# Five weight pieces' lower parts made by TensorE, three short units' lower parts all on VectorE, and a smaller DMA scratch for GpSimd

## The chip, the core and the metric

One core of a Trainium2 chip runs the whole program. The metric is the device time of one execution in microseconds (us): 898.3 us for the kernel before, the median of three runs (898.18, 898.3 and 901.01). One further execution was taken by the hardware profiler; all rows come from that one.

Engines are named as in the profile: PE is TensorE's matmul and PEld its weight load, DVE is VectorE, ACT is ScalarE, POOL is GpSimd, SP issues most DMAs.

## What is computed

Three layers follow each other: a linear attention with a complex decay, a feed-forward layer, and a mixture of 8 experts of which each token takes one.

```python
for t in range(S):                                  # B, H, S, D = 4, 8, 768, 48
    S_re, S_im = ar*S_re - ai*S_im + k[t] v[t]^T, ar*S_im + ai*S_re
    y[:, :, t] = einsum('bhd,bhde->bhe', q[t], S_re)
x = y.transpose(0, 2, 1, 3).reshape(3072, 384)
h = x @ w_in                                        # 384 -> 2048
x = (max(h, 0) + alpha * min(h, 0)) @ w_out         # 2048 -> 384
e = argmax(x @ w_gate + modality_bias[modality_id]) # 8 experts
out[token] = gate * (max(x @ w1[e], 0) @ w2[e])     # 384 -> 1024 -> 384
```

The feed-forward weights come as 64-bit floats and are put together from their two halves on the chip.

## The kernel before

**Two parts per number.** The two feed-forward layers multiply in a format narrower than float32 (F32R). Each operand is split: an upper part (rounded by a copy on ACT) and a lower part (the operand less the upper part). A product is the sum of three matmuls: upper by upper, upper by lower, lower by upper.

**Weight pieces.** `w_in` and `w_out` are cut into 16 pieces of 128 hidden channels, fc = 0 to 15, each 128 x 768: 384 columns of `w_in` and 384 of `w_out`. A piece is loaded as raw bits (`wraw`), decoded by three DVE instructions (L624, L627, L630) into a working buffer (`wf`), copied to the upper part by ACT (L577), and subtracted by DVE to give the lower part (L578). PE transposes the `w_out` half into a PSUM bank (`pl`, L582), ACT copies it out (L586), and `weights_gate` multiplies it by `w_gate` (`og`, L596). There are four working buffers, chosen by fc % 4, so piece fc + 4 can be decoded only when all readers of piece fc are done. The banks for `pl`, `og` and the attention's `py` and `pu` are given out in turn from one pair (`pq0`, `pq1`).

**Attention.** A step k (24 of them, 128 time steps of one batch row) begins with `polar`: magnitudes, angles and three running scans on DVE and ACT, ending in the rows `z` (L785, L787). These are written to DRAM and read back in another layout (`zd`, `qk`); then PE multiplies (`pa`, `pk`, `py`, `pu`, L818 to L850). Two steps make a unit.

**First feed-forward layer** (`moe1`). For each of 12 units, 8 groups p of two pieces: `ph` on PE (L887, L888 upper, L890 with the weights' lower part), the activation `n` (ACT L895, DVE L897), its upper part `gh` (ACT L900), its lower part `gl` (DVE L875), then `acc` (PE L930). Below, `ph0_4` is group 4 of unit 0. There are two `ph` banks, so a group can begin only when `n` of the group two before it is done.

**Order at the start.** Two strings set the order in which the parts of the first units are written. START is run before `moe1` begins, TURN has one entry for each of its first turns. A letter is a step: x, y, q, p are single instructions of `polar` of steps 0, 1, 2-3 and 4-5; A, a, B and C are parts of attention; D decodes two pieces and F makes their parts; f is four matmuls on the identity that fill PE's time (L191); < and > begin and end a stretch in which each step's DVE instructions are chained behind the last. A scheduler then places the instructions on each engine's queue; every queue runs in order.

**Experts** (`moe2`). The tail of the program. Tokens are gathered by POOL (L377), multiplied unit by unit and scattered by POOL (L413). A unit has 8 steps f; step f needs 768 columns of weights, loaded into one of a few buffers (`wr`, four here), copied by ACT (`wh`, L485) and subtracted for the lower part (`wl`, L486): by POOL for f = 0, 3, 6 and by DVE for the others. Units of 128 x nt tokens: four with nt = 4 (`s`), one with nt = 3 (`t`), three with nt = 2 (`f`, the last). `hh` and `hl` are the two parts of the hidden values (L504, L505), `ptf` the transposes at the head of the next unit (L390).

Of the kernel before, what the change touches and what calls it, by code (L numbers as in the profile page):

```python
# [11 lines left out]
F32 = mybir.dt.float32  # L12
F32R = mybir.dt.float32r
# [3 lines left out]
ALU = mybir.AluOpType  # L17
PSUM = bass.MemoryType.PSUM

B, H, S, D = 4, 8, 768, 48  # L20
# [3 lines left out]
DM, FF = 384, 2048  # L24
# [3 lines left out]
F2 = 8  # L28
# [6 lines left out]
NEARLY = 4  # L35
NFINAL = 3
NTRIP = 1
START = 'x3 y2 x3 y3 x y x y x y3 < x3 y2 x < x4 > x2 y > x3 < x y2 < x2 q b y10 c w A2 a A > r f a A f a f a < > q f2 q8 f2 q5 D F q3 r f q2 f q9 f q3 f q4 D d'
TURN = ('B', 'D2 B F2 B > B2 D F B', 'B2 D F2 L', '', 'D', 'D F p', '', 'p3 F', '<2 p > p2', 'p > p3 < p3 > p11', 'p7', '', 'p4 < C3', 'C3 >2 s >', 'C p C')
GHB = 3  # L40
ATB = 2
LEAD = 3
# [57 lines left out]
class Emit:  # L100
# [26 lines left out]
    def consts(self):  # L127
        nc, cp = self.nc, self.cp
        self.tiny = cp.tile([128, 1], F32, name="tiny")
        nc.vector.memset(self.tiny, 1e-25)  # L130
        warm = cp.tile([128, 1], F32, name="warm")
        nc.scalar.activation(warm, self.tiny, AF.Abs_reciprocal_sqrt)
        self.trig = cp.tile([128, 1], F32, name="trig")
        self.ident = cp.tile([128, 128], F32, name="ident")
        make_identity(nc, self.ident)
        self.mask = cp.tile([128, 128], F32, name="mask")
        nc.gpsimd.memset(self.mask, 1.0)
        nc.gpsimd.affine_select(
            out=self.mask, in_=self.mask, pattern=[[1, 128]], compare_op=ALU.is_ge,
            fill=0.0, base=0, channel_multiplier=-1,  # L140
        )
        self.hpi = cp.tile([128, 1], F32, name="hpi")
        nc.gpsimd.memset(self.hpi, math.pi / 2)
        self.mth = cp.tile([128, 1], F32, name="mth")
        nc.gpsimd.memset(self.mth, -0.56)

        self.first = {}
        for nm, at0, rest in (("angle", 0.0, 1.0), ("inverse", 1.0, 1e18), ("decay", 1.0, 0.0)):
            t = self.first[nm] = cp.tile([128, 3 * CH], BF16, name=f"first_{nm}")
            nc.gpsimd.memset(t, rest)  # L150
            nc.gpsimd.memset(t[:, ::CH], at0)
        self.carry = cp.tile([128, B, 3], F32, name="carry")
        self.magic = cp.tile([128, 1], F32, name="magic")
        nc.gpsimd.memset(self.magic, MAGIC)

        self.oks = cp.tile([128, NSTEP], F32, name="oks")
        nc.gpsimd.memset(self.oks, 2.0 * 3 * CH)
        self.pend = cp.tile([128, NSTEP, 3], F32, name="pend")
        self.state = cp.tile([96, B * H * D + 16], F32, name="state")
        nc.gpsimd.memset(self.state[:, B * H * D:], 0.0)  # L160
        self.al1 = cp.tile([128, NFC], F32, name="al1")
        one = self.one = cp.tile([128, 1], F32, name="one")
        nc.gpsimd.memset(one, 1.0)
        self.mhalf = cp.tile([128, 1], F32, name="mhalf")
        nc.gpsimd.memset(self.mhalf, -0.5)
        self.ones = one.to_broadcast([128, CH])
        self.small = cp.tile([128, NFC], F32, name="small")
        nc.gpsimd.memset(self.small, 0.0)
# [251 lines left out]
    def moe2(self, units):  # L420


        n = len(units)
        regs, heads, turned, accs, ws, hs, gates = {}, {}, {}, {}, {}, {}, {}

        def head(j):
            if j < n:
                nm, get, nt, known = units[j]
                regs[j] = get()
                heads[j] = self.unit_head(nm, regs[j][1], nt, known)  # L430

        def load(i):
            j, f = divmod(i, F2)
            if j < n:
                ws[i] = self.ffn_load(units[j][0], regs[j][0], f)

        def turn(j):
            if j < n:
                turned[j] = self.unit_turn(units[j][0], units[j][2], heads[j][1])

        def l2(i):
            j, f = divmod(i, F2)
            nm, _, nt, _ = units[j]
            if f == 0:
                accs[j] = self.ffn_acc(nm, nt)
            self.ffn_l2(nt, f, hs.pop(i), accs[j])
            if f == F2 - 1:
                self.unit_out(nm, nt, heads.pop(j)[0], gates.pop(j), accs.pop(j))

        head(0)  # L450
        for i in range(PF):
            load(i)
        yield
        turn(0)
        yield
        for i in range(n * F2):
            j, f = divmod(i, F2)
            nm, _, nt, _ = units[j]
            if f == HD:
                head(j + 1)  # L460
            load(i + PF)
            hs[i] = self.ffn_l1(nm, nt, f, ws.pop(i), turned[j])
            if f == GT:
                gates[j] = self.unit_gate(nm, nt, heads[j][1])
            if f == F2 - 1:
                turn(j + 1)
            for k in {0: [i - 1], 1: [], F2 - 1: [i - 2, i - 1]}.get(f, [i - 2]):
                if k >= 0:
                    l2(k)
            yield  # L470
        l2(n * F2 - 1)
        yield
# [1 line left out]
    def ffn_acc(self, nm, nt):  # L474
        return [self.pq.tile([128, DM], F32, name=f"a2{nm}_{t}", tag="a2", bufs=4) for t in range(nt)]

    def ffn_load(self, nm, e, f):

        nc, hp = self.nc, self.hp
        raw = hp.tile([128, 2 * DM], F32, name=f"wr{nm}_{f}", tag="wr", bufs=self.hb[0])  # L480
        nc.sync.dma_start(raw, self.wcat[ds(e, 1), f].rearrange("o p n -> p (o n)"))
        wh = hp.tile([128, 2 * DM], F32R, name=f"wh{nm}_{f}", tag="wh", bufs=self.hb[1])
        wl = hp.tile([128, 2 * DM], F32R, name=f"wl{nm}_{f}", tag="wl", bufs=self.hb[1])
        with self.behind_turn(PM):
            nc.scalar.copy(wh, raw)  # L485
            (nc.vector if f % 3 else nc.gpsimd).tensor_tensor(wl, raw, wh.bitcast(F32), ALU.subtract)  # L486
        return wh, wl

    def ffn_l1(self, nm, nt, f, w, xT):
# [75 lines left out]
    def weights_part(self, *fcs, guard=False):  # L565

        nc = self.nc
        if 0 in fcs:
            self.w, self.wT = [], {}
        ws = [self.tmp(fc) for fc in fcs]  # L570
        yield from self.decode([self.raws.pop(fc) for fc in fcs], ws, guard)
        yield
        for fc, w in zip(fcs, ws):
            p = self.wp.tile([128, 2, WW], F32R, name=f"w{fc}", tag=f"w{fc}")
            self.w.append(p)
            n = 2 * DM
            nc.scalar.copy(p[:, 0, :n], w)  # L577
            nc.vector.tensor_tensor(p[:, 1, :n], w, p[:, 0, :n].bitcast(F32), ALU.subtract)  # L578
            pool, tag, bufs = self.bank()
            pt = pool.tile([128, 512], F32, name=f"pl{fc}", tag=tag, bufs=bufs)  # L580
            for c in range(3):
                nc.tensor.transpose(pt[:, 128 * c:128 * c + 128], w[:, DM + 128 * c:DM + 128 * c + 128], self.ident)  # L582
            if fc % 4 == 0:
                self.wT4 = self.ap_.tile([128, 4, DM], F32, name=f"wT{fc}", tag="z", bufs=ZB)
            wT = self.wT[fc] = self.wT4[:, fc % 4]
            nc.scalar.copy(wT, pt[:, :DM])  # L586
# [584 lines left out]
def body(ctx, tc, aps):  # L1171
# [5 lines left out]
    def polar(*ks):  # L1177
        st = third if ks[0] == 4 else em.polar(ks)
        for k in ks:
            em.load_v(k)  # L1180
        yield
        yield from em.polar_run(st, 0, len(ks), True)
        yield
# [25 lines left out]
    def attn_unit(u):  # L1209
        xts[u] = em.wp.tile([128, 3, 2, 256], F32R, name=f"xt{u}", tag="xt", bufs=XB)  # L1210
        for k in (2 * u, 2 * u + 1):
            yield from em.attn(k, xts[u])
# [78 lines left out]
    def steps(text):  # L1291

        for part in re.findall("([^0-9 ]+)([0-9]*)", text):
            for c in part[0] * int(part[1] or 1):
                if c in "<>":
                    link[0] = c == "<"
                else:
                    with em.behind_turn() if c in PT else nullcontext():
                        (chained if link[0] else step)(c)

    gens["p"], gens["C"] = polar(4, 5), attn_unit(2)
    steps(START)
    jobs, later = {}, {}
# [21 lines left out]

    for g, text in enumerate(TURN):
        first, _, then = text.partition("/")
        at(g, steps, first)
        at(g, steps, then, d=later)
    at(CG, consts, d=later)  # L1330
    shift = {0: 0}
    for u in range(3, NU):
# [153 lines left out]
```

## Time and profile before

| | |
|---|---|
| median of three runs | 898.3 us |
| the profiled execution's own time | 894.0 us |
| its span, first to last instruction | 892.2 us |
| PE, DVE busy | 821.8 us (92%), 669.9 us (75%) |
| ACT, POOL busy | 467.2 us (52%), 205.2 us (23%) |
| mean granted TensorE clock | 0.979 of full speed |

A matmul counts as busy while it streams or waits in the array's pipeline, so a busy PE can still be a slow one. A wait is booked on the engine that idles, with the instruction that ended it.

### The profile page before, as it was taken

To read this page: it belongs to the slowest core of one execution; us is meant where nothing else is said; L and a number is where in the kernel's file an instruction comes from. 1 tells how busy PE (TensorE), PEld (TensorE's weight loads), DVE (VectorE), ACT (ScalarE), POOL (GpSimd) and SP (SyncE) were. 2 spreads that over 40 slices of the span, in tenths; PEclk is the share of its full clock that TensorE was granted. 3 is DMA by queue.
4 is the path that set the end of the run, shared out by engine and by line. 5 is a ranking of instruction groups with operands and counts; after the bars stand their busy time and mean duration, and the time that the engine had idled before them with its cause. 6 is when DMAs were issued, how large, how long until landed. Compare 5 with 4: busy or idle time off the path is not lost.

```text
span 892.2 us, 16224 instructions
## 1 busy us (share of the span) xinstructions
PE 821.8 (92%) x6037; PEld 784.8 (88%) x6037; DVE 669.9 (75%) x1419; ACT 467.2 (52%) x871; POOL 205.2 (23%) x204
## 2 busy tenths in 40 slices
PE   0699998999799999999999999899999999999993
PEld 0688997989799999999999999899988888999893
DVE  7999978999886979797988889355644754656751
ACT  7644466757564656474656554133344445456550
POOL 2001321021120121212121211000332543534640
PEclk9999899999899999999999999899999999999997
DMA  8769203662737253443535262401365477667650
GB/s 337 244 214 329 35 1 107 156 207 72 192 67 192 68 141 119 114 134 100 144 99 126 104 154 95 85 24 27 105 188 144 144 235 257 199 229 268 203 170 20
DMA packets 63591, 130.37 MB, mean 146 GB/s; under 512 B 10456, under 2 KB 39656, under 8 KB 63504
## 3 DMA queue, kind: packets, MB, share of 16 engines
q1 hardware_dynamic: 59536, 119.49, 44.9%
q0 software_dynamic: 3968, 9.77, 3.3%
q8 instruction: 49, 0.80, 0.4%
q14 instruction: 38, 0.31, 0.1%
HBM read 98.17 MB, written 28.91 MB: 142 GB/s over the span
## 4 chain that ended last, share of the span: by engine, by line
PE 53%; DVE 22%; DMA 12%; issue 6%; ACT 3%; POOL 2%; SPq 1%; POOLq 0%; ACTq 0%; DVEq 0%
PE acc L930 12%; PE a2s L516 6%; DMA qk<-zd 6%; PE ph L887 5%; PE ph L888 4%; PE ph L890 4%; PE pa L818 3%; DVE n L897 2%; PE p2s L501 2%; PE p2s L497 2%; PE p2s L498 2%; DMA zd<-z 2%; DVE z L785 2%; PE pu L850 2%; PE py L836 2%
## 5 line engine op out<-in xcount | busy, mean ns | idle before, releaser
L930 PE MATMUL acc<-w,gh 128*128 128x392 f32 x768 | 158.8, 345 | 0.3 <-ACT gh L900 0.3
L887 PE MATMUL ph<-xt,w 128*128 128x256 f32 x576 | 153.8, 295 | 5.2 <-DVE n L897 4.2
L888 PE MATMUL ph<-xt,w 128*128 128x256 f32 x576 | 148.0, 285 | 0.0
L930 PEld LDWEIGHTS acc<-w,gh 128*128 128x128 f32 x768 | 133.7, 190 | 1.0 <-ACT gh L900 0.5
L887 PEld LDWEIGHTS ph<-xt,w 128*128 128x128 f32 x576 | 110.9, 192 | 7.1 <-DVE n L897 4.8
L897 DVE SCALAR_TENSOR_TENSOR n<-n,al,ph 128x256 f32<-128x256 f32 x192 | 84.1, 474 | 42.2 <-ACT n L895 42.1
L888 PEld LDWEIGHTS ph<-xt,w 128*128 128x128 f32 x576 | 111.1, 193 | 0.2 <-issue 0.2
L890 PE MATMUL ph<-xt,w 128*128 128x256 f32 x576 | 102.1, 286 | 0.0
L895 ACT ACTIVATE n<-ph 128x512 f32<-128x512 f32 x96 | 57.0, 594 | 82.1 <-PE ph L890 80.0
L875 DVE TENSOR_TENSOR gl<-n,gh 128x512 fp32r<-128x512 f32 x96 | 66.8, 696 | 31.1 <-ACT gh L900 30.9
L900 ACT CAST gh<-n 128x512 fp32r<-128x512 f32 x96 | 59.2, 617 | 57.9 <-DVE n L897 53.3
L930 PE MATMUL acc<-w,gl 128*128 128x392 f32 x384 | 89.3, 347 | 0.0
L890 PEld LDWEIGHTS ph<-xt,w 128*128 128x128 f32 x576 | 83.5, 192 | 0.0
L279 POOL DMA_INDIRECT tbl<-tok,ix x24 | 27.4, 1143 | 203.1 <-DVE ix L277 193.7
L930 PEld LDWEIGHTS acc<-w,gl 128*128 128x128 f32 x384 | 70.4, 192 | 0.3 <-issue 0.2
L818 PE MATMUL pa<-qk 96*128 96x128 f32 x384 | 54.3, 285 | 13.6 <-DMA qk<-zd 11.7
L818 PEld LDWEIGHTS pa<-qk 96*128 96x128 f32 x384 | 50.1, 197 | 17.4 <-issue 8.9
L505 DVE SCALAR_TENSOR_TENSOR hls<-p2s,hhs 128x512 fp32r<-128x512 f32 x32 | 22.1, 690 | 33.3 <-ACT hhs L504 29.3
L836 PE MATMUL py<-at,v 128*64 128x128 f32 x384 | 42.4, 286 | 2.0 <-DVE at L820 2.0
L516 PE MATMUL a2s<-whs,hhs 128*128 128x384 f32 x128 | 43.8, 342 | 0.0
L516 PE MATMUL a2s<-wls,hhs 128*128 128x384 f32 x128 | 43.5, 340 | 0.0
L485 ACT CAST whs<-wrs 128x768 fp32r<-128x768 f32 x32 | 26.4, 835 | 30.5 <-PE a2s L516 17.1
(363 smaller groups left out, 1898.1 us busy)
## 6 DMA issues: line engine op xcount, KB each, us to landing
zd<-z SPq DMA_DIRECT2D x24, 771.0 KB
qk<-zd SPq DMA_DIRECT2D x24, 771.0 KB
wraw<-in_w_io_dram SPq DMA_DIRECT2D x16, 768.0 KB
wrs<-in_wcat_dram SPq DMA_DIRECT2D x32, 384.0 KB
ck<-in_w_io_dram SPq DMA_DIRECT2D x16, 768.0 KB
wrf<-in_wcat_dram SPq DMA_DIRECT2D x24, 384.0 KB
wa<-in_pa__dram SPq DMA_DIRECT2D x10, 768.0 KB
wq<-in_pq__dram SPq DMA_DIRECT2D x10, 768.0 KB
```

Source lines behind the costliest of these rows:

```text
L279: nc.gpsimd.indirect_dma_start(out=self.tbl, out_offset=bass.IndirectOffsetOnAxis(ap=ix, axis=0), in_=self.tok[:, c, b, :], in_offset=None ...
L516: nc.tensor.matmul(acc[t], x[:, 128 * t:128 * t + 128], w[:, DM:], start=(f == 0 and x is hh and w is wh), stop=(last and x is hl))
L818: nc.tensor.matmul(pa[:, i, :], kt[:, h, :], qt[:, h, :CH], start=True, stop=True)
L836: nc.tensor.matmul(o, v[:, h * D:h * D + 64], ats[g][:, i, :], start=True, stop=(c == 0))
L875: return engine.tensor_tensor(gl, nf, gh.bitcast(F32), ALU.subtract).ins
L887: nc.tensor.matmul(ph[:, i, :], w1(fc, 0, c), xt[:, c, 0, :], start=(c == 0), stop=False)
L888: nc.tensor.matmul(ph[:, i, :], w1(fc, 0, c), xt[:, c, 1, :], start=False, stop=False)
L890: last = nc.tensor.matmul(ph[:, i, :], w1(fc, 1, c), xt[:, c, 0, :], start=False, stop=(c == 2)).ins
L895: nc.scalar.activation(nf, ph, AF.Relu, scale=-1.0)
L897: paced = nc.vector.scalar_tensor_tensor(nf[:, i, :], nf[:, i, :], self.al1[:, 2 * p + i:2 * p + i + 1], ph[:, i, :], ALU.mult, ALU.add).ins
L900: copy = nc.scalar.copy(gh, nf).ins
L930: nc.tensor.matmul(acc[t][:, :XW], x[:, i, 128 * t:128 * t + 128], self.w[2 * p + i][:, h, DM:], start=(p == i == h == 0 and x is gh), sto ...
```

## The change

Four edits. (1) For pieces fc = 3 to 7 the lower part is no longer made by DVE: PE multiplies the piece by the identity (float32, L586 after), adds the upper part times minus identity (F32R, L587 after) into the same bank (`pd`), and ACT copies the difference out (L588 after), in two halves of 384 columns. (2) START and TURN are rewritten. (3) In units with nt under 3 the weights' lower parts for f = 0, 3, 6 are made by DVE too. (4) The SBUF that POOL's DMAs use for descriptors is set to 4096 bytes of a partition.

```diff
-START = 'x3 y2 x3 y3 x y x y x y3 < x3 y2 x < x4 > x2 y > x3 < x y2 < x2 q b y10 c w A2 a A > r f a A f a f a < > q f2 q8 f2 q5 D F q3 r f q2 f q9 f q3 f q4 D d'
+START = 'x2 y x y4 x3 y x2 y x y3 x7 y > x2 < y > x2 y x2 <2 x y3 < x2 q b y2 r y7 c w A2 f a A > r a A f a f a < > q2 f2 q8 f2 q f q3 D F q3 f q8 f q8 f2 q2'
...
+        self.minus = cp.tile([128, 128], F32R, name="minus")
+        nc.gpsimd.tensor_scalar(self.minus, self.ident, -1.0, 0.0, ALU.mult, ALU.add)
...
-            (nc.vector if f % 3 else nc.gpsimd).tensor_tensor(wl, raw, wh.bitcast(F32), ALU.subtract)
+            (nc.vector if f % 3 or nt < 3 else nc.gpsimd).tensor_tensor(wl, raw, wh.bitcast(F32), ALU.subtract)
...
-            nc.vector.tensor_tensor(p[:, 1, :n], w, p[:, 0, :n].bitcast(F32), ALU.subtract)
+            if 3 <= fc < 8:
+                for i in range(2):
+                    cs = slice(DM * i, DM * i + DM)
+                    pool, tag, bufs = self.bank()
+                    pd = pool.tile([128, 512], F32, name=f"pd{fc}_{i}", tag=tag, bufs=bufs)
+                    nc.tensor.matmul(pd[:, :DM], self.ident, w[:, cs], start=True, stop=False)
+                    nc.tensor.matmul(pd[:, :DM], self.minus, p[:, 0, cs], start=False, stop=True)
+                    nc.scalar.copy(p[:, 1, cs], pd[:, :DM])
+            else:
+                nc.vector.tensor_tensor(p[:, 1, :n], w, p[:, 0, :n].bitcast(F32), ALU.subtract)
...
-    nc = _bacc.Bacc("TRN2", target_bir_lowering=False, num_devices=1)
+    nc = _bacc.Bacc("TRN2", target_bir_lowering=False, num_devices=1, dynamic_dma_scratch_size=4096)
```

In the order of the queues, lines past L137 are shifted by up to 12 after the change (L578 is L590, L624 is L636, L818 is L830). A number behind a name is the piece, step or unit.

DVE's queue from attention step 2 on, before:

```order
L820 TENSOR_TENSOR at2_0_550<-pa2_0_545,mask_85 128x512
L578 TENSOR_TENSOR w2_627<-wf2_520,w2_627 128x768
L578 TENSOR_TENSOR w3_635<-wf3_521,w3_635 128x768
L624 TENSOR_SCALAR wf6_605<-wraw6_245 128x768
L624 TENSOR_SCALAR wf7_606<-wraw7_247 128x768
L627 SCALAR_TENSOR_TENSOR wf6_605<-wraw6_245,wf6_605 128x768
L627 SCALAR_TENSOR_TENSOR wf7_606<-wraw7_247,wf7_606 128x768
L630 SCALAR_TENSOR_TENSOR wf6_605<-wraw6_245,wf6_605 128x768
L630 SCALAR_TENSOR_TENSOR wf7_606<-wraw7_247,wf7_606 128x768
L820 TENSOR_TENSOR at2_1_618<-pa2_1_613,mask_85 128x512
L578 TENSOR_TENSOR w4_643<-wf4_597,w4_643 128x768
L578 TENSOR_TENSOR w5_652<-wf5_598,w5_652 128x768
```

and after:

```order
L832 TENSOR_TENSOR at2_0_556<-pa2_0_551,mask_87 128x512
L636 TENSOR_SCALAR wf7_612<-wraw7_249 128x768
L590 TENSOR_TENSOR w2_633<-wf2_526,w2_633 128x768
L639 SCALAR_TENSOR_TENSOR wf7_612<-wraw7_249,wf7_612 128x768
L636 TENSOR_SCALAR wf6_611<-wraw6_247 128x768
L642 SCALAR_TENSOR_TENSOR wf7_612<-wraw7_249,wf7_612 128x768
L639 SCALAR_TENSOR_TENSOR wf6_611<-wraw6_247,wf6_611 128x768
L832 TENSOR_TENSOR at2_1_624<-pa2_1_619,mask_87 128x512
L642 SCALAR_TENSOR_TENSOR wf6_611<-wraw6_247,wf6_611 128x768
L636 TENSOR_SCALAR wf8_771<-wraw8_251 128x768
L636 TENSOR_SCALAR wf9_772<-wraw9_253 128x768
L639 SCALAR_TENSOR_TENSOR wf8_771<-wraw8_251,wf8_771 128x768
```

The subtractions of pieces 3, 4 and 5 are gone from here (those of 6 and 7 from further on), and the decoding of pieces 8 and 9 stands in their place.

PE's queue at the same place, before:

```order
L818 MATMUL pa2_0_545<-qk2_516 128x128 x4
L826 MATMUL pk2_0_552<-ident_80,qk2_516 128x96 x4
L582 MATMUL pl4_646<-ident_80,wf4_597 128x128 x3
L887 MATMUL ph0_2_845<-xt0_151,w4_643 128x256
L582 MATMUL pl5_655<-ident_80,wf5_598 128x128 x3
L826 MATMUL pk2_1_620<-ident_80,qk2_516 128x96 x3
L818 MATMUL pa2_1_613<-qk2_516 128x128 x4
```

and after:

```order
L838 MATMUL pk2_0_558<-ident_80,qk2_522 128x96 x4
L586 MATMUL pd4_0_658<-wf4_603,ident_80 128x384
L587 MATMUL pd4_0_658<-w4_656,minus_85 128x384
L838 MATMUL pk2_1_626<-ident_80,qk2_522 128x96 x3
L830 MATMUL pa2_1_619<-qk2_522 128x128 x4
L838 MATMUL pk2_1_626<-ident_80,qk2_522 128x96
L586 MATMUL pd4_1_662<-wf4_603,ident_80 128x384
L587 MATMUL pd4_1_662<-w4_656,minus_85 128x384
L594 MATMUL pl4_666<-ident_80,wf4_603 128x128 x3
L838 MATMUL pk3_0_720<-ident_80,qk3_524 128x96 x3
L586 MATMUL pd5_0_674<-wf5_604,ident_80 128x384
L587 MATMUL pd5_0_674<-w5_672,minus_85 128x384
```

Each of the five pieces puts four matmuls into PE's queue, between the attention's own, and `pl` of a piece stands behind them.

DVE's queue at the end of `polar` of steps 4 and 5, before:

```order
L897 SCALAR_TENSOR_TENSOR n1_3_1396<-n1_3_1396,al1_109,ph1_3_1377 128x256 x2
L875 TENSOR_TENSOR gl0_6_1402<-n0_6_1347,gh0_6_1351 128x512
L875 TENSOR_TENSOR gl1_3_1454<-n1_3_1396,gh1_3_1400 128x512
L785 TENSOR_TENSOR z4_1373<-wq4_541,x4_1028 128x3x128
L787 TENSOR_TENSOR z4_1373<-wq4_541,x4_1028 128x3x128
```

and after:

```order
L909 SCALAR_TENSOR_TENSOR n1_3_1437<-n1_3_1437,al1_111,ph1_3_1418 128x256 x2
L887 TENSOR_TENSOR gl0_6_1443<-n0_6_1388,gh0_6_1392 128x512
L797 TENSOR_TENSOR z4_1414<-wq4_547,x4_1059 128x3x128
L799 TENSOR_TENSOR z4_1414<-wq4_547,x4_1059 128x3x128
L797 TENSOR_TENSOR z5_1462<-wq4_547,e4_1061 128x3x128
```

`gl1_3` no longer stands ahead of the last two instructions of `z4`.

## Rows read from the trace of the kernel before

**Rows 1.** The page's head: span of the profiled execution.

```profile
span 892.2 us, 16224 instructions
```

**Rows 2.** Stretches of the span: busy time by engine, granted clock, DMA share.

```profile
core 0: us, PE busy (x) PEld busy (x) DVE busy (x) ACT busy (x) POOL busy (x), PEclk, DMA share, GB/s
...
60.00:100.00 40.00, 36.01 (x282) 32.77 (x282) 39.73 (x61) 20.36 (x47) 6.33 (x11) 0.92 0.78 249
100.00:162.00 62.00, 57.14 (x389) 56.12 (x388) 53.95 (x81) 40.52 (x76) 11.94 (x22) 0.94 0.22 64
162.00:660.00 498.00, 483.59 (x3883) 468.01 (x3882) 396.87 (x944) 262.18 (x472) 86.05 (x71) 0.99 0.42 112
...
820.00:892.20 72.20, 56.40 (x390) 54.51 (x389) 34.75 (x67) 30.42 (x63) 29.77 (x21) 0.93 0.41 129
```

**Rows 3.** PE's three largest waits, 60 to 162 us: total, times, longest.

```profile
PE ph L887 <- DVE n L897: 4.2, 1, 4.2
PE py L836 <- DVE at L820: 2.0, 2, 1.6
PE pl L582 <- DVE wf L630: 1.2, 1, 1.2
```

**Rows 4.** Timeline of DVE: start, us, work, and idle time before it in brackets.

```profile
94.18 3.58 DVE L578 TENSOR_TENSOR w<-wf,w 128x768 fp32r<-128x768 f32 x4
...
122.55 0.95 DVE L698 TENSOR_TENSOR m<-m,e 128x768 f32<-128x768 f32 x1
...
141.03 0.46 DVE L897 SCALAR_TENSOR_TENSOR n<-n,al,ph 128x256 f32<-128x256 f32 x1
...
149.31 0.69 DVE L875 TENSOR_TENSOR gl<-n,gh 128x512 fp32r<-128x512 f32 x1 [1.89 <-ACT gh L900]
...
150.39 0.56 DVE L787 TENSOR_TENSOR z<-wq,x 128x384 f32<-128x384 f32 x1
```

**Rows 5.** Timeline of PE.

```profile
51.24 3.80 PE L191 MATMUL fill<-ident 128*128 128x128 f32 x32
...
96.63 2.11 PE L596 MATMUL og<-wg,wT 128*128 128x8 f32 x12
...
141.54 0.45 PE L887 MATMUL ph<-xt,w 128*128 128x256 f32 x1 [4.15 <-DVE n L897]
```

**Rows 6.** The chain that ended last: an F32R stretch, a POOL DMA, attention's way back.

```profile
746.35 2.10 PE a2s L516 x12
...
699.25 3.91 DMA tbl<-tok,ix
...
154.53 6.65 DMA qk<-zd
161.22 1.16 PE pa L818 x8
```

**Rows 7.** ACT's copies out of a bank, by line: ns min/median/max.

```profile
L586 ACT COPY wT<-pl x16: 473/482/496, 55.4 to 117.7; 128x384 f32<-128x384 f32 x16
```

**Rows 8.** PE's waits from 162 us to the end: total, times, longest.

```profile
PE pa L818 <- DMA qk<-zd: 11.7, 6, 5.1
PE ptf L390 <- DVE hlf L505: 2.1, 1, 2.1
```

**Rows 9.** Timelines of POOL, ACT and DVE in the short units.

```profile
831.50 4.38 POOL L486 TENSOR_TENSOR wlf<-wrf,whf 128x768 fp32r<-128x768 f32 x2
...
843.87 1.58 POOL L377 DMA_INDIRECT xgf<-x2d,idsf  x1
...
836.51 0.83 ACT L485 CAST whf<-wrf 128x768 fp32r<-128x768 f32 x1 [3.37 <-DMA wrf<-in_wcat_dram]
...
842.73 1.81 DVE L486 TENSOR_TENSOR wlf<-wrf,whf 128x768 fp32r<-128x768 f32 x1 [1.08 <-ACT whf L485]
...
868.88 0.96 DVE L486 TENSOR_TENSOR wlf<-wrf,whf 128x768 fp32r<-128x768 f32 x1 [1.09 <-ACT whf L485]
```

**Rows 10.** POOL's scatters by line: ns min/median/max.

```profile
L413 POOL DMA_INDIRECT out_dram<-ots,idss x16: 976/1038/1823, 692.1 to 803.3; - x16
```

More of the change, by code (lines that the diff above doesn't have):

```diff
@@ L37 @@
 NTRIP = 1
-START = 'x3 y2 x3 y3 x y x y x y3 < x3 y2 x < x4 > x2 y > x3 < x y2 < x2 q b y10 c w A2 a A > r f a A f a f a < > q f2 q8 f2 q5 D F q3 r f q2 f q9 f q3 f q4 D d'
-TURN = ('B', 'D2 B F2 B > B2 D F B', 'B2 D F2 L', '', 'D', 'D F p', '', 'p3 F', '<2 p > p2', 'p > p3 < p3 > p11', 'p7', '', 'p4 < C3', 'C3 >2 s >', 'C p C')
+START = 'x2 y x y4 x3 y x2 y x y3 x7 y > x2 < y > x2 y x2 <2 x y3 < x2 q b y2 r y7 c w A2 f a A > r a A f a f a < > q2 f2 q8 f2 q f q3 D F q3 f q8 f q8 f2 q2'
+TURN = ('D d B >', 'D2 B F2 B3 > F B D B', 'D L', 'D F2', 'D F', 'p', '', 'p3 F p < p < p', 'p2 >', 'p3 < p2 B p6 > p6', 'p6', 'p3', '< p C3', 'C3 >2', 'C p C s >')
 GHB = 3
@@ L434, in load @@
             if j < n:
-                ws[i] = self.ffn_load(units[j][0], regs[j][0], f)
+                ws[i] = self.ffn_load(units[j][0], regs[j][0], f, units[j][2])
         def turn(j):
@@ L475, in ffn_acc, with ffn_load @@
         return [self.pq.tile([128, DM], F32, name=f"a2{nm}_{t}", tag="a2", bufs=4) for t in range(nt)]
-    def ffn_load(self, nm, e, f):
+    def ffn_load(self, nm, e, f, nt=4):
         nc, hp = self.nc, self.hp
```

## The prediction

> **What bounds the kernel now.** I read the windows first, then PE's waits, then the timelines, and the chain of waits last. The windows [rows 2] show two regimes. From 162 to 660 us PE is busy 483.59 of 498 us while DVE is busy 396.87: PE is the limit, at a clock of 0.99. From 60 to 100 us it is the other way round: DVE is busy 39.73 of 40 us, PE 36.01, and DVE stays close to full to 162 us (53.95 of 62). PE's waits say the same. In 60 to 162 us its largest waits [rows 3] are 4.2, 2.0 and 1.2 us, 7.4 in sum, and all end with a DVE instruction. After 162 us PE waits for attention's rows, six times, 11.7 us [rows 8]. Each such wait is a DMA that starts when DVE has finished `polar`, and stands on the chain [rows 6] (6.65 us of DMA, then `pa` at 161.22). So what moves DVE's work and PE's together at about 160 us moves the end with it, as PE has almost no slack behind.
>
> The tail (820 us on) has one PE wait, 2.1 us, for `hlf` of DVE [rows 8]. Its origin is on POOL [rows 9]: behind scatters and gathers it begins the lower parts of the short units only at 831.50; the raw buffer comes free late, ACT's copy waits 3.37 us for the load into it, and DVE and PE follow.
>
> **The front: pieces 3 to 7 (edits 1 and 2).**
>
> *What DVE loses.* Four of the subtractions take 3.58 us (at 94.18) [rows 4], 0.9 each; one follows the next by some 0.87. Five are 4.35 us. The queue after the change holds the same DVE instructions otherwise, so from attention step 4 on DVE has 4.35 us less ahead of it. The new order gives more to some places: `gl1_3` (at 149.31, 0.69 us after 1.89 us idle) [rows 4] no longer stands ahead of `z4`'s last instruction, and `polar` of steps 4 and 5 (122.55) has some 6 us less work ahead, by the instructions that now stand behind it. What is moved behind is done later, so I count the 4.35 alone. DVE is full where they are taken away, so nothing hides them.
>
> *What PE gains.* Ten float32 products of 384 columns and ten F32R ones. "f2 q8 f2" in START is sixteen identity matmuls of 128 columns; they show as 32 records in 3.80 us [rows 5], two records of 119 ns each, 0.24 us a matmul. Three such are 0.71 us, ten times 7.1. The F32R product is priced by the chain's `a2s`, 12 of 384 columns in 2.10 us [rows 6], 0.175 each, 1.75 in sum. Together 8.9 us. If a float32 product cost only two F32R ones it would be 3.5 + 1.75 = 5.25: the lower bound. I take 8.9, since the fill is the same operation on the same operand types.
>
> *Does PE have room?* From 60 to 162 us PE is busy 36.01 + 57.14 = 93.15 of 102 us [rows 2]. With 8.85 more it would be busy 102.0, which leaves nothing. But the stretch contains time at the lower clock: 0.92 and 0.94 are means of 2.4 and 1.2 GHz, so 40 x 0.08 + 62 x 0.06 = 6.9 us of busy time is there only because the clock was halved. It falls behind the waits named above and behind the 24 products of 8 columns around 95 us, where twelve take 2.11 us [rows 5]. The change spreads those in sixes between larger matmuls, and fills PE's gaps before them with 384-column ones. If all of that clock comes back, PE needs 102.0 - 6.9 = 95.1 us, and a stretch shortened by 4.35 offers 97.65. So it fits, narrowly; I take it that most of the clock returns. The `n` wait of 4.15 us at 141.54 [rows 5] shrinks by as much as DVE comes earlier than PE there.
>
> *What ACT gains.* Ten copies of 128x384 at 0.48 us [rows 7], 4.8 us; ACT is busy 20.36 of 40 us in 60 to 100 [rows 2], so they have room, but each stands between PE's product and the next user of its bank. There are two banks for `pd`, `pl`, `py` and `pu`. Nothing in the trace before shows this hand-off more than once over 0.3 us, so its cost is bounded: nothing below, and above one 0.83 us cast ahead in ACT's queue (at 836.51) [rows 9] and the 0.48 us copy, 1.3 us for each of the ten halves, 13 us. PE has attention's or `ph`'s instructions between most halves, so I take nothing and keep the rest as a rival. A piece's working buffer is now freed by PE rather than DVE, one to three microseconds later; the decoding of the piece four further on waits for it on DVE, with DVE's whole queue behind. At most this adds to the same rival.
>
> The additional fills, 4 matmuls or 0.95 us, lie before `ph` of unit 0 in a place where PE waits for the pieces anyway. `minus` is one early POOL instruction off any path; POOL is 23% busy.
>
> Sum of the front: -4.35 us, with bounds of -7.4 (PE's three waits on DVE go whole) and 0 (PE full, with what goes beyond it among the rivals).
>
> **The tail (edit 3).** The nine lower parts of the three short units go from POOL to DVE. One takes DVE 0.96 us undisturbed (868.88) and POOL about 2.19 (4.38 for two) [rows 9]. On DVE the first is done by about 830, the raw buffer comes free 3 us sooner, and the 2.1 us wait has nothing to end it late. DVE is busy 34.75 of 72.2 us from 820 on [rows 2]; nine more are 8.6, so it has room. I take -2.1; bounds are 0 and -2.5 (the wait and half a microsecond of its wake).
>
> What speaks against this is in the same rows: DVE's lower part took 1.81 us where POOL ran its own beside it (842.73) and 0.96 alone, and POOL's gather took 1.58 us at 843.87, right after. The Trainium skill (SBUF — State Buffer, "SBUF: two separate sides") states why such pairs collide: VectorE with two SBUF inputs and a GpSimd operation that reads SBUF share a port pair as an exclusive lock, and the one that starts second is fully blocked. By that rule the nine subtractions, each now at the head of a unit beside POOL's gathers, would hold those off too; by the row the collision is with POOL's own subtraction, which goes away. The row is what I go by: with two gathers held off by 0.56 us each (1.58 less the 1.02 of an ordinary one, as the scatters of rows 10 have in the median) the tail would come to -1.0 in place of -2.1, and the whole to 893.0, inside A.
>
> **The scratch (edit 4).** It removes and adds no instruction. Where POOL has to wait for descriptors of an earlier transfer, a gather or scatter would start later: the trace before shows them at 0.98 to 1.82 us [rows 10] and a transfer behind one at 3.91 [rows 6]. I take nothing; the upper bound is three unit heads in the tail held by the landing of the transfer before, 3 x 3.91 less some 2 us of slack each (an estimate from PE's step of twelve `a2s`, 2.10 [rows 6]), about +6. It is rival D.
>
> **Sum.** -4.35 - 2.1 = -6.4 us. The profiled execution's own time is 894.0 (span 892.2 [rows 1] and 1.8 around it); it would be 887.6. The median of the runs, 898.3, lies 4.3 above the profiled one; I keep that offset, so the predicted time is 898.3 - 6.4 = **891.9 us**. About 0.3%, or 2.7 us, is what a measurement of this kernel can tell from no change: faster is below 895.6, slower above 901.0.
>
> **The rivals.**
>
> *A, the forecast*: -6.4; its bounds together give 898.3 - 7.4 - 2.5 = 888.4 at the low end, and the tail at -1.0 with half the front 895.1 at the high one. For it: DVE at 39.73 of 40 and three waits on DVE. Against it: PE fits only if the clock returns. Chance 0.56.
>
> *B, PE takes what DVE gives*: PE's 8.9 us are paid by half of the 7.4 us of waits and half of the 6.9 of clock, 7.15, so the front is +1.7 and the tail -2.1: 897.9, no change that can be told. The same time results if the front does not do what it says because PE's waits there end with a load and not with DVE; DMA share is 0.78 from 60 to 100 us [rows 2]. Chance 0.16.
>
> *C, PE becomes the bound* between 64 and 95 us: the products come in before `ph0_3`, the clock does not return, and PE's queue waits at the two banks for ACT's copies. PE: +8.85, less 3.7 of waits filled, tail -2.1, gives +3.0: **901.4**, slower; with all waits left, +6.75 or 905. It decides without any hand-off if no clock returns; if half of the 6.9 us returns, from hand-offs of 3.1 us, 0.3 for each half piece; if all, from 6.5 us, 0.65 each. For it: 102.0 of 102 us. Against it: PE waits 4.2 us in one place after all this, at 137 to 141, and can catch up there. Chance 0.17, of it 0.04 within the bound.
>
> *D, the scratch delays POOL's transfers*: +6 less the rest's -1.0 or so, 903, decided by whether more descriptors are outstanding than it holds. The trace can't exclude it. The Trainium skill (DMA: Bandwidth & Descriptors, "Terms") says that descriptors of GpSimd's transfers are written to rings in SBUF, so fewer bytes are a shorter ring; no run so far shows one full. Chance 0.03.
>
> *E, both effects in full*: all 7.4 us of waits and the idle 1.89 of `gl1_3` go, and PE keeps the full clock to 162 us: -7.4 - 1.9 - 2.1 = -11.4: 886.9. Chance 0.08.
>
> **How the numbers follow.** Faster is A and E, 0.64; same is B (0.15) and 0.04 of C, 0.19; slower is the rest, 0.17. The range of 8 in 10 is from 886.9 (E) to 901.4 (C at its price); what lies outside is D, C beyond its price and the tail of E. A alone is 888.4 to 895.1.
>
> **What would show it.** In the profile after: eleven subtractions in place of sixteen at the line of DVE's lower part; `polar` 4's first instruction (122.55 before) at 115 to 119; `pa` after `zd` (161.22) at 156 to 157; PE's wait for `n` gone or under 2 us; a granted clock above 0.95 in 60 to 100; no wait of `ptf` for `hlf`; no lower parts of `f` units on POOL. The forecast is wrong if PE is at 100% from 64 to 106 us with the clock still low (B or C), if new waits of `pd` or `pl` for ACT sum to over 3 us (C), if `pa` is not before 159 (B), or if POOL's gathers grow past 2 us (D).

## The result, and the profile after

The changed kernel takes **882.65 us** (median of 4 runs, 881.87 to 885.25); the kernel before took 898.24 us beside it (4 runs, 897.81 to 901.01). The ratio is 0.983, with a 95% interval of 0.980 to 0.986: 15.6 us faster. A second series, beside other runs of the kernel before, gave 0.984 (0.981 to 0.988). The forecast was 891.9 with a range of 886.9 to 901.4; the direction was right, and the time lies 4 us below the range.

The profiled execution of the changed kernel has a span of 883.5 us, 8.7 less than before [rows 1]. Its head, then the same stretches as in [rows 2]:

```profile
span 883.5 us, 16307 instructions
```

```profile
core 0: us, PE busy (x) PEld busy (x) DVE busy (x) ACT busy (x) POOL busy (x), PEclk, DMA share, GB/s
60.00:100.00 40.00, 39.20 (x288) 33.93 (x288) 36.28 (x56) 23.74 (x53) 1.57 (x6) 0.96 0.74 249
100.00:162.00 62.00, 61.11 (x453) 59.51 (x452) 57.75 (x89) 44.29 (x85) 22.99 (x26) 1.00 0.29 84
162.00:660.00 498.00, 482.55 (x3871) 467.60 (x3871) 392.75 (x942) 259.62 (x468) 88.93 (x71) 0.99 0.43 111
820.00:883.50 63.50, 55.71 (x391) 54.50 (x389) 38.97 (x75) 30.91 (x63) 16.25 (x13) 0.96 0.47 148
```

The front has changed sides. PE is busy 100.3 of 102 us from 60 to 162 us (93.15 before), at a clock of 0.96 and 1.00 (0.92 and 0.94), and DVE has 3.7 us of idle time in the first stretch, where it had 0.3. PE's waits in 60 to 162 us, which were 7.4 us on DVE in the three largest alone [rows 3], are these, all of them:

```profile
PE pl L594 <- ACT wT L598: 0.6, 1, 0.6
PE ph L899 <- ACT w L579: 0.6, 1, 0.6
PE pa L830 <- DMA qk<-zd: 0.3, 1, 0.3
PE pl L594 <- DVE wf L642: 0.2, 1, 0.2
```

The chain's pieces that answer to the last rows of [rows 6] come 3.6 to 4.2 us sooner: `zd` at 146.80 (151.01), and `pa` at 157.59 (161.22). First the piece of before, then those of after:

```profile
151.01 3.51 DMA zd<-z
```

```profile
146.80 3.51 DMA zd<-z
150.33 7.22 DMA qk<-zd
...
157.59 1.16 PE pa L830 x8
```

The other place is the very end. POOL's last scatter, in its timeline before and after (start, us, in brackets the idle time before it):

```profile
880.20 0.98 POOL L413 DMA_INDIRECT out_dram<-otf,idsf  x1 [0.31 <-issue]
```

```profile
877.40 0.97 POOL L415 DMA_INDIRECT out_dram<-otf,idsf  x1 [0.30 <-issue]
```

Before, the span ran on for 12.0 us from that start (to 892.2); after, for 6.1 (to 883.5). What changed in there is mainly one instruction on POOL's sequencer, which counts as no busy time and stands in none of the rows ahead of the prediction. The program's last line, all instructions of the kind DRAIN on POOL (ns min/median/max), before and after:

```profile
L1482 POOLq DRAIN  x3: 40/107/6123, 885.2 to 891.9; - x3
```

```profile
L1494 POOLq DRAIN  x3: 40/107/978, 881.7 to 883.2; - x3
```

One DRAIN takes 6.12 us before and 0.98 after. The profile's waits show the same time under another name: SP's queue waits 5.6 us "for PE's sequencer" in the closing barrier before, and 0.5 after. PE had long been done; the row of the instruction itself tells it.

**The sum by places** in the two profiles, each from the start of an instruction to that of the next: to the last `acc` by the upper part in the first feed-forward layer, from 656.2 to 653.2, -3.0; from there to the first `a2f` of the short units +3.2 (169.7 to 172.9); the short units -3.0 (51.9 to 48.9); last product to last scatter 0; end -5.9. Together -8.7. The +3.2 belongs to this one execution: its clock is 0.83 from 700 to 720 us. A second profile of the same program was taken to try this; it shows 1.00 there and 170.1 us for the stretch. Its span was 874.4 where 880 to 881 had been expected, so the clock is not all that differs. The spread between executions sits mainly in PE's waits for `qk` after 162 us (11.7 us before, 12.4 after, 7.5 in that second profile), and it doesn't follow the edits: from 7.5 to 13.1 us in seven profiles with the changed front, 10.0 to 11.7 in three with that of before. So below, stages are compared by marks that these waits don't move, and whole times by ratios.

### The profile page after: what moved, and what is told of

It is laid out like the page before. It is cut to its first block, busy times and chain, and to the rows that moved or that the text cites. A ratio compares the mean times of both kernels' runs of the same rounds, so it can differ in the third digit from the quotient of the medians.

```text
span 883.5 us, 16307 instructions
## 1 busy us (share of the span) xinstructions
PE 825.5 (93%) x6075; PEld 786.8 (89%) x6075; DVE 669.1 (76%) x1423; ACT 471.4 (53%) x881; POOL 198.3 (22%) x196
## 4 chain that ended last, share of the span: by engine, by line
PE 63%; DVE 18%; DMA 9%; issue 5%; ACT 2%; POOL 2%; SPq 1%; POOLq 0%; DVEq 0%; ACTq 0%
PE acc L942 14%; PE a2s L518 7%; PE ph L899 5%; DMA qk<-zd 5%; PE ph L902 5%; PE ph L900 5%; PE pa L830 4%; DMA zd<-z 3%; PE p2s L503 2%; PE pu L862 2%; PE p2s L499 2%; PE p2s L500 2%; PE py L848 2%; DVE n L909 2%; PE a2f L518 2%
## 5 line engine op out<-in xcount | busy, mean ns | idle before, releaser
L899 PE MATMUL ph<-xt,w 128*128 128x256 f32 x576 | 151.9, 292 | 2.0 <-issue 0.8
L900 PE MATMUL ph<-xt,w 128*128 128x256 f32 x576 | 146.3, 283 | 0.0
L899 PEld LDWEIGHTS ph<-xt,w 128*128 128x128 f32 x576 | 109.5, 190 | 3.3 <-issue 1.9
L900 PEld LDWEIGHTS ph<-xt,w 128*128 128x128 f32 x576 | 109.6, 190 | 0.2 <-issue 0.2
L902 PE MATMUL ph<-xt,w 128*128 128x256 f32 x576 | 100.8, 283 | 0.0
L942 PE MATMUL acc<-w,gl 128*128 128x392 f32 x384 | 87.2, 342 | 0.0
L902 PEld LDWEIGHTS ph<-xt,w 128*128 128x128 f32 x576 | 82.4, 190 | 0.0
L281 POOL DMA_INDIRECT tbl<-tok,ix x24 | 29.4, 1225 | 202.5 <-DVE ix L279 192.7
L830 PE MATMUL pa<-qk 96*128 96x128 f32 x384 | 54.1, 285 | 15.5 <-DMA qk<-zd 13.2
L830 PEld LDWEIGHTS pa<-qk 96*128 96x128 f32 x384 | 50.3, 197 | 18.9 <-issue 8.8
L832 DVE TENSOR_TENSOR at<-pa,mask 128x512 f32<-128x512 f32 x48 | 32.7, 682 | 12.8 <-PE pa L830 6.3
```

The costliest lines, as they stand in the source:

```text
L281: nc.gpsimd.indirect_dma_start(out=self.tbl, out_offset=bass.IndirectOffsetOnAxis(ap=ix, axis=0), in_=self.tok[:, c, b, :], in_offset=None ...
L830: nc.tensor.matmul(pa[:, i, :], kt[:, h, :], qt[:, h, :CH], start=True, stop=True)
L832: self.last = nc.vector.tensor_tensor(at, pa, self.mask.unsqueeze(1).to_broadcast([128, 4, CH]), ALU.mult).ins
L899: nc.tensor.matmul(ph[:, i, :], w1(fc, 0, c), xt[:, c, 0, :], start=(c == 0), stop=False)
L900: nc.tensor.matmul(ph[:, i, :], w1(fc, 0, c), xt[:, c, 1, :], start=False, stop=False)
L902: last = nc.tensor.matmul(ph[:, i, :], w1(fc, 1, c), xt[:, c, 0, :], start=False, stop=(c == 2)).ins
```

## The experiments

Twelve kernels ran, in three groups of four, each group beside the kernel before on one chip (medians of before: 893.29, 892.91 and 892.46 us). "pa" is the start of the eight products at 161.22 before, the mark of the front; "short units" is the time between the starts of the first and the last `a2f` of the upper parts; "end" is from the last scatter's start to the end of the span.

| kernel | ratio (95% interval) | pa | short units | end | DRAIN |
|---|---|---|---|---|---|
| before | 1 | 161.22 | 51.9 | 12.0 | 6.12 |
| changed | 0.983 (0.980 to 0.986) | 157.59 | 48.9 | 6.1 | 0.98 |
| changed, again | 0.984 (0.981 to 0.988) | 157.83 | 48.9 | 5.6 | 0.98 |
| before + scratch | 0.992 (0.990 to 0.994) | 162.63 | 52.3 | 5.8 | 0.98 |
| before + short units | 0.995 (0.994 to 0.997) | 162.07 | 49.0 | 12.6 | 6.12 |
| before + front | 0.997 (0.995 to 0.999) | 158.00 | 54.2 | 12.1 | 6.12 |
| changed, scratch as before | 0.989 (0.987 to 0.991) | 155.94 | 48.9 | 12.1 | 6.12 |
| changed, short units as before | 0.988 (0.986 to 0.991) | 158.16 | 55.0 | 5.8 | 0.98 |
| changed, no piece by TensorE | 0.985 (0.982 to 0.988) | 158.71 | 48.9 | 5.7 | 0.98 |
| changed, order of before | 0.988 (0.985 to 0.991) | 164.54 | 48.9 | 5.9 | 0.98 |

**The scratch alone.** Edit: the kernel before with `dynamic_dma_scratch_size=4096`.

> The kernel before with edit 4 alone (scratch 4096). Theory S: the scratch shortens what comes behind the last scatter of POOL. In the profile of before 11.0 us lie between the end of the last scatter (881.18) and the end of the span (892.2), after the change 5.1 us (878.37 to 883.5); so this kernel gains 5.9 us, the stretch behind the last scatter is 5.1 us and everything ahead of it is as before within 1 us. Rival N, as forecast: the edit costs and gains nothing, the stretch is 11 us and the time is within 1 us of before; the 5.9 us would then come from the lower parts or the order. Rival D: gathers and scatters wait, slower by 4 us or more.

885.36 us against 893.29, 0.992: -7 us, between -5.5 and -8.8 by the interval. Theory S holds: the DRAIN row is that of the changed kernel, the end is 5.8 us, and front and short units are as before (to 1.4 and 0.4 us, where 1 was expected). 5.1 us of it is the DRAIN; the other 1.0 lies between the last scatter's start and the first instruction of the closing barrier (4.9 us before, 3.9 here). That part is there in all the profiles (to POOL's first DRAIN 5.0 to 5.6 us with the scratch of before, 3.7 to 4.3 with 4096 bytes); what it consists of is not known.

```profile
L1482 POOLq DRAIN  x3: 40/107/978, 884.4 to 886.0; - x3
```

**The scratch taken out of the changed kernel.**

```diff
-num_devices=1, dynamic_dma_scratch_size=4096)
+num_devices=1)
```

> The changed kernel without edit 4 (scratch as before). Theory S: 5.9 us slower than the changed kernel, 0.989 of before by the medians (about 888.5), with 11 us behind the last scatter. Rival N: as fast as the changed kernel, 0.983 (about 882.7).

0.989, as theory S says, and the DRAIN is 6123 ns again. Of the four edits, the two runs share only this one.

```profile
L1494 POOLq DRAIN  x3: 40/107/6123, 874.5 to 881.2; - x3
```

**Its size.** 8192 and 1024 bytes in place of 4096.

> The changed kernel with a scratch of 8192 bytes. Theory S2: POOL's DRAIN at the end grows with the scratch in proportion to its bytes: it took 6123 ns with 16384 and 978 ns with 4096, 0.429 us for each 1024 bytes more, so 978 + 4 x 429 = 2.7 us here. Rival: a step (either 1.0 or 6.1 us), which would say that something else than the size decides.

> The changed kernel with a scratch of 1024 bytes. Theory S2: the DRAIN of 978 ns shrinks to its constant part, under 0.3 us, so 0.5 to 1 us faster than the changed kernel if the gathers and scatters still find room. Rival D of the prediction: with a quarter of the room POOL waits for descriptors, gathers and scatters take over 2 us each in place of 1.0 to 1.2 (tbl, xgs, out_dram), and the kernel is slower than the changed one by 4 us or more.

```profile
L1494 POOLq DRAIN  x3: 40/107/2122, 873.0 to 875.7; - x3
```

```profile
L1494 POOLq DRAIN  x3: 40/107/652, 877.7 to 879.0; - x3
```

It is no step, so the size decides; but it isn't proportional either. 652, 978, 2122 and 6123 ns for 1, 4, 8 and 16 KiB: 0.11 us a KiB at first, 0.29, then 0.50. Theory S2 forecast 2.7 for 8 KiB and was too high, and under 0.3 for 1 KiB and too low. Rival D fell: with 1024 bytes the gathers and scatters take what they took (means 1.04 to 1.40 us for the kinds, 1.04 to 1.40 in the changed kernel), and the kernel runs at 0.985 (0.983 to 0.988). That is the changed kernel's time within the interval, so the 0.3 us that it could still give can't be seen. The kernel with 8192 bytes ran once (877.7 us against 892.46), so for it the DRAIN is the evidence and not the time.

**The short units alone**, and taken out of the changed kernel.

```diff
-(nc.vector if f % 3 or nt < 3 else nc.gpsimd)
+(nc.vector if f % 3 else nc.gpsimd)
```

> The kernel before with edit 3 alone (short units' lower parts all on VectorE). Theory: PE's wait of 2.1 us for hlf goes, the time falls by 2 to 3 us, and the stretch behind the last scatter stays at 11 us. Rival: the nine subtractions on VectorE are paid elsewhere (gathers held off, hlf late), less than 1 us gained. Rival N of the run before: this edit also shortens the end, 8 us or more gained.

> The changed kernel without edit 3 (POOL makes three lower parts of each short unit again). Theory: the 2.1 us wait of PE for hlf is back, 2 to 3 us slower than the changed kernel, about 885; stretch behind the last scatter 5 us. Rival: the wait does not come back in this order, as fast as the changed kernel.

Alone it gives 0.995, -4.2 us by the ratio (-2.7 to -5.7), where 2 to 3 had been forecast; the mark shows 2.9 of it: the 2.1 us wait for `hlf` is gone, and each later unit is shorter by another 0.26 and 0.45 us (18.20 to 17.94 and 21.23 to 20.78 between `ptf` of one unit, `ptf` of the next, and the last product), waits too short to head a list. In the changed kernel the edit is worth more than the 2 to 3 us of the theory: without it the ratio is 0.988 in place of 0.983 or 0.984, some 4 us. Two waits stand there, and the short units take 55.0 us:

```profile
PE ptf L392 <- DVE hlf L507: 2.5, 1, 2.5
PE p2f L499 <- DVE hlf L507: 1.3, 1, 1.3
```

**The front alone**, and its two halves.

> The kernel before with edits 1 and 2 alone (five pieces by TensorE, new order; scratch and short units as before). Theory: 4.35 us of DVE leave the queue ahead of 160 us and PE has room: the first pa behind the DMA of qk starts 3 to 5 us sooner (161.2 before), the end of the first feed-forward layer 3 to 5 us sooner, the time falls by 3 to 6 us (ratio about 0.995); DRAIN of POOL at the end stays at 6.1 us. Rival B: PE takes what DVE gives, under 1.5 us gained. Rival N2: the front is worth 8 us or more, since the sum of the two parts measured alone (0.8% and 0.5%) leaves about 0.5% of the changed kernel's 1.7%, and it could also be that the parts don't add up.

890.27 us against 892.91, 0.997: -2.6 us. `pa` comes at 158.00, 3 to 4.5 us sooner than in the three kernels with the old front (161.22, 162.63, 162.07), as the theory says. The whole time shows less than the 3 to 6 us forecast (the interval, 1.0 to 4.6, reaches into them). In its profile the short units lose 2.3 us (54.2 for 51.9, with a wait of 2.8 us for `hlf`), which would account for it; but that profile is of the slowest of 14 runs, 897.26 us. With edit 3 beside it the short units take 48.9.

The changed kernel with `if False:` in place of `if 3 <= fc < 8:`, so that DVE makes all sixteen lower parts in the new order:

> The changed kernel without edit 1: its order of steps, but DVE makes all sixteen lower parts. Theory: DVE has its 4.35 us again ahead of 160 us, so some 3 to 5 us slower than the changed kernel, PE waits for DVE again between 60 and 162 us (4 us or more in sum, 1.7 in the changed kernel). Rival O: the order of steps alone brings the front's gain, under 1 us slower than the changed kernel.

The changed kernel with START and TURN of before, so that TensorE makes five pieces in the old order:

> The changed kernel with the order of steps of before (edit 2 undone; five pieces still made by TensorE). Theory: the products stand in PE's queue where PE had little room, and the order spreads them; without it PE and DVE wait for each other and part of the gain goes, 1 to 4 us slower than the changed kernel. Rival P: the moved work alone brings all, as fast as the changed kernel within 1 us. Rival C of the prediction: PE becomes the bound, slower than the changed kernel by 5 us or more.

| `pa`, us | old order | new order |
|---|---|---|
| DVE makes all | 161.97 (mean of 3) | 158.71 |
| PE makes five | 164.54 | 157.37 (mean of 7) |

Kernels with the same front spread over 1.4 us in the left column and 2.2 in the right one, and two cells are one profile each. So the 1.3 us between the two cells of the right column isn't settled; the other differences go beyond the spread. The move of work alone makes `pa` **2.6 us later**; the order alone makes it 3.3 us earlier; both together 4.6 us.

The whole times say the same. Without the five pieces the kernel takes 879.75 us beside the changed one's 878.21: 1.5 us, and the intervals overlap (0.985 and 0.984). The theory (3 to 5 us slower, 4 us or more of waits) named the wrong engine too: PE's waits are 5.6 us in sum there, but only 2.3 of them end with DVE. Rival O, under 1 us, is nearer. So in the new order nothing can be told of what the five pieces give. With the order of before it takes 882.26, 4.1 us slower, as its theory says (1 to 4); rival P falls, and rival C's 5 us is not reached. In that order PE, at 38.49 of 40 us, is fuller than DVE from 60 to 100 us, the half of rival C that came true; the clock, which C kept low, is 0.96 there. The windows and waits of that kernel (old order, five pieces by PE):

```profile
60.00:100.00 40.00, 38.49 (x291) 33.78 (x290) 35.69 (x55) 23.18 (x52) 2.41 (x6) 0.96 0.79 255
100.00:162.00 62.00, 57.28 (x401) 56.62 (x401) 52.94 (x81) 39.59 (x77) 14.01 (x25) 0.94 0.18 56
```

```profile
PE ph L899 <- DVE n L909: 4.1, 1, 4.1
```

DVE has lost its subtractions and is idle 4.3 of the first 40 us, as it now waits for attention's products (2.5 us on PE, 1.5 on ACT's copy of one); PE still has the same 4.1 us wait for `n` at the other end, behind `polar`. The new order shortens that wait by itself (1.4 us in the kernel with no piece by TensorE).

**How many pieces.** `if 3 <= fc < 5:` and `if 3 <= fc < 11:`, two and eight pieces by TensorE in place of five.

> The changed kernel with two pieces by TensorE in place of five (fc = 3 and 4). Theory Q: PE is full from 60 to 106 us, each half piece costs it 0.85 us, and most of the front's gain is the order's; two pieces lie between none (1.5 us slower than the changed kernel) and five, within 1.5 us of the changed kernel. Rival R: DVE is still the bound, each piece gives 0.87 us, so 2.6 us slower.

> The changed kernel with eight pieces by TensorE in place of five (fc = 3 to 10). Theory Q: PE is already full from 60 to 162 us (100.3 of 102 us), six more half pieces at 0.85 us are 5.1 us on PE with nothing to take their place, so 2 to 5 us slower than the changed kernel. Rival R: DVE is the bound, each piece gives 0.87 us, so 2.6 us faster.

Two pieces: 0.985 (0.982 to 0.987), `pa` at 157.52, the same as five. Eight: 0.990 (0.988 to 0.992), some 5 us slower than five, `pa` at 163.57. Theory Q holds, at the upper end of its 2 to 5 us; rival R falls both times: the third to fifth piece give nothing that can be seen, and the sixth to eighth cost. The price on PE can be read from the changed kernel's timeline, where two halves of a piece and what follows stand at the higher clock (start, us):

```profile
76.25 0.63 PE L587 MATMUL pd<-w,minus 128*128 128x384 f32 x1
76.72 0.81 PE L586 MATMUL pd<-wf,ident 128*128 128x384 f32 x2
77.07 0.64 PE L587 MATMUL pd<-w,minus 128*128 128x384 f32 x1
77.54 0.49 PE L594 MATMUL pl<-ident,wf 128*128 128x128 f32 x3
```

From one start to the next: 0.35 us for the float32 product, 0.47 for the F32R one behind it. That is 0.82 us a half piece.

## Why the prediction was wrong

**The scratch is the step that failed.** The prediction says of it: "It removes and adds no instruction", and "I take nothing", with an upper bound and none below. Measured: -5.1 us on one DRAIN and 1.0 more ahead of it. The row was in the trace before, and so was the gap of which it fills 6.1 us: the last scatter ends at 881.18, the span at 892.2 [rows 1], 11.0 us that no engine's busy time and no piece of the chain covers. I took "no instruction changes" for "no time changes", and asked only what a smaller scratch could delay. With -6.0 in the sum the forecast would have been 885.9, and the range would have held the result.

**What DVE loses: right in sum by luck, wrong in its parts.** -4.35 us were forecast for the front, and `pa` moved from a mean of 161.97 to 157.37, -4.6, just short of the 156 to 157 that was named. But the sum was argued from five subtractions, with nothing for the order. The step "DVE is full where they are taken away, so nothing hides them" is refuted: taken away alone, they make `pa` 2.6 us late. The order that I counted at nothing is -3.3.

**PE's room: right.** "So it fits, narrowly": PE is busy 100.3 of 102 us. The clock came back where it was needed (0.96 from 60 to 100 us, 1.00 in all of 100 to 162; the 8-column products stand apart, but in groups of twelve as before and not in sixes), and with eight pieces it fits no more. In the same order without the pieces the clock from 60 to 100 us is 0.87, and PE's waits are 5.6 us for 1.7: the products fill time that PE otherwise waits or works slowly. The price of 8.9 us was close to the 8.2 at the higher clock by luck, from two wrong terms: the float32 product is 0.35 us and not 0.71, and the F32R one behind it 0.47 and not 0.175.

**ACT's copies: right.** No wait of `pd` for ACT stands in PE's list; `pl` waits 0.6 us, once, as before.

**The tail: right mechanism, mis-sized.** -2.1 was forecast with a bound of -2.5; it is -3.0, as two more units each lose less than half a microsecond that the list of waits had not shown. The rule of the Trainium skill (SBUF — State Buffer, "SBUF: two separate sides"), by which the moved subtractions would hold off the gathers there, didn't decide the time: the gathers of the short units take 1.13 us in the mean after and 1.17 before. POOL's scatters beside the subtractions did lengthen, two of them to 1.8 us where 1.0 is ordinary; the three of the unit with nt = 3 take 1.40 us in the mean in every kernel with edit 3, and 1.10 in every one without. No wait of PE follows from it.

```profile
829.28 1.75 POOL L415 DMA_INDIRECT out_dram<-ott,idst  x1 [0.31 <-DVE hlf L507]
...
843.11 1.82 POOL L415 DMA_INDIRECT out_dram<-otf,idsf  x1 [0.30 <-issue]
```

**The signs.** Of those named, these held: eleven subtractions, no wait of `ptf`, no POOL lower parts in short units, the `n` wait gone, and the clock. `polar` 4 began at 120.13 and not at 115 to 119: 2.4 us of the gain are there at that point, and 1.8 more come between it and `zd`.

**The rest.** The marks add up to -4.6 - 3.0 - 5.9 = -13.5 us, 0.985 of before; the measured -15.6 lies 2 us beyond, and the interval of the ratio (-12.7 to -17.8) holds the sum; where those 2 us come from, if they are real, stays open. The two profiles alone show only -8.7, since that of before lies 4.3 us below its runs' median and that of after 2.6 above. The chance of B stands as 0.16 in one place and as 0.15 in another.

## What to carry to other kernels

Before costing anything, subtract the last busy instruction from the end of the span: what is left is a term too, and sequencer instructions such as DRAIN are read by the program's last line, not from busy time; a setting that changes no instruction can change the duration of one. Moving work from a full engine to one that was 91% busy gave nothing by itself here, and little or nothing on top of the new order, which brought most of the front's gain: price a move on the receiver, and test the move and the order apart. Where executions of one program differ by as much as the effect (874.4 and 883.5 us of span here), read the parts from marks that the scattering waits don't move.

## What the hardware showed that was not expected

A POOL instruction on 128x8 elements, 0.35 us in the median, took up to 4.13 us. The rows of that line on POOL in the changed kernel (ns min/median/max), its place in the timeline (a pair, then the slow one by itself), and what DVE did then:

```profile
L614 POOL TENSOR_TENSOR w<-of,w x16: 192/349/4132, 64.7 to 146.3; 128x8 fp32r<-128x8 f32 x16
```

```profile
138.47 4.99 POOL L614 TENSOR_TENSOR w<-of,w 128x8 fp32r<-128x8 f32 x2 [9.10 <-ACT w L613]
143.42 2.42 POOL L799 TENSOR_TENSOR z<-wq,e 128x384 f32<-128x384 f32 x2
```

```profile
139.33 4.13 POOL L614 TENSOR_TENSOR w<-of,w 128x8 fp32r<-128x8 f32 x1
```

```profile
138.42 0.95 DVE L760 TENSOR_TENSOR_SCAN s<-first_inverse,s 128x384 f32<-128x384 bf16 x1
139.28 0.46 DVE L909 SCALAR_TENSOR_TENSOR n<-n,al,ph 128x256 f32<-128x256 f32 x1
139.66 0.68 DVE L887 TENSOR_TENSOR gl<-n,gh 128x512 fp32r<-128x512 f32 x1
140.26 0.95 DVE L760 TENSOR_TENSOR_SCAN m<-first_decay,m 128x384 f32<-128x384 bf16 x1
141.13 0.93 DVE L786 TENSOR_TENSOR wq<-wq,s 128x768 f32<-128x768 f32 x1
141.98 0.95 DVE L788 TENSOR_TENSOR wq<-wq,m 128x768 f32<-128x768 f32 x1
142.84 0.55 DVE L797 TENSOR_TENSOR z<-wq,e 128x384 f32<-128x384 f32 x1
143.31 0.86 DVE L909 SCALAR_TENSOR_TENSOR n<-n,al,ph 128x256 f32<-128x256 f32 x2
```

From 139.66 to 143.39 DVE runs operations with two operands in SBUF without a gap, and the small one on POOL, begun at 139.33, ends at 143.46, behind the last of them. The rule of the Trainium skill (SBUF — State Buffer, "SBUF: two separate sides") says that such a pair excludes each other for a whole instruction. The trace agrees at the end of that stretch; at its start the `n` at 139.28, which has one operand in a PSUM bank, did not let the small one in. That DVE's stream of such instructions is what held it was not tried by itself. The pair stands just ahead of POOL's part of `z`, so it may cost the front time; no run shows how much. And the DRAIN: from 4 to 16 KiB of scratch it grows 6.3-fold, more than the bytes do.
